# The forward pass of an attention and MLP block: moved loads, reordered copies and filler products at chunk boundaries

## The chip, the cores and the metric

The kernel runs on one core of a Trainium2 chip. The metric is the device time of one execution in microseconds; the time of a kernel is the median of its runs. The engines named below are TensorE (PE: matrix products into PSUM; PEld is its weight load), VectorE (DVE), ScalarE (ACT), GpSimd (POOL) and SyncE (SP). Each engine works through its own instruction stream in order and waits on semaphores. DMAs are issued from the streams of SP and POOL (and ACT in the backward pass).

## The reference

The reference is a transformer block with adaptive layer norm and its gradient: the kernel must return the block's output and the gradients of nine inputs.

```python
mod = (silu(c) @ w_mod).reshape(1, 6, 1, 512)              # sa, ca, ga, sb, cb, gb
h = layernorm(x) * (1 + ca) + sa
x = x + ga * attention(h, wqkv, wo)                        # 32 heads of 16, 2048 tokens, softmax
h = layernorm(x) * (1 + cb) + sb
x = x + gb * (relu(h @ w1 + b1)**2 @ w2 + b2)              # 512 -> 1792 -> 512
out, grads = vjp(block)(grad_out)                          # dx, dwqkv, dwo, dw1, db1, dw2, db2, dc, dw_mod
```

## The kernel before

The program has a short preparation, a forward stage, a stretch that finishes the last chunk, and a backward stage over attention. The change lies in the forward stage alone.

**Units.** Attention scores are computed for 32 heads in 8 groups of 4 (`hg`), the 2048 queries in 4 chunks of 512 (`qc`), the keys in 16 tiles of 128 (`kt`). One unit is one (`qc`, `hg`, `kt`), so there are NF = 512 units, and group boundaries are at the multiples of 16 and chunk boundaries at the multiples of 128. In unit u, `fscore(u)` (line 557) issues four score products on PE into two PSUM pairs `psST` and two exponentials `ET` of 128x1024 on ACT. `fpv(u - 2)` (line 572) issues the four products with the values into the one PSUM bank `oacc`; when a group ends (`kt` = 15, seen in unit `kt` = 1 of the next group) DVE copies `oacc` to `ostage`, POOL casts that to `obf`, and SP later moves rows to `rrows` and a turned copy to `O_un`.

**What is woven in.** `step(u)` (line 1114) adds at most one further product per unit, all through one PSUM bank (`mm()`, tile `pm`): the next piece of `dense_chunk` (line 317), a generator that runs output projection, layer norm, MLP and their backward products for the chunk whose attention has just ended, or one "chain" of weight gradients from the queue `dwq` (`add_chain`, line 226). A number that the generator yields is a count of units to wait. Where a unit has no product, `steady` (line 603) adds two products with zeros, except in the last tile of a group.

**Due times.** `later(lag, f, ...)` puts an issue off by a number of units; `run_due` issues it at the start of its unit. This sets the place of an instruction in its engine's stream, and nothing more: an engine runs on ahead of the units when nothing in its stream makes it wait. DMAs of one queue that use the same one of eight semaphores wait for each other, so each DMA on POOL waits for the landing of the eighth before it.

**Row loads.** `fload` (line 549) loads the keys (`kt_sb`, four DMAs), the queries (`qt_sb`, four) and a bound per query (`m_st`, one) for the next group on the POOL queue, one DMA per unit in chunks 1 to 3, beginning at `kt` = 4 (line 1154). The first score product of the group waits for the last of them.

**A chunk's start.** `ffinish` (line 661), called at the end of unit 8 of the next chunk, turns the softmax sums on PE, and DVE takes their reciprocal and scales four tiles `O_c`. `chunk_loads` (line 282) issues the loads of the chunk's weights and gradients and plans `scaled` (line 305), which multiplies four tiles on POOL into `gf`, whose turned copy `gfT` SP makes.

**Output projection** (lines 345 to 352): four products into `pm`, one per token tile, each followed on DVE by a copy into `a_c`, by `with_input` (two operations) and by `stats` (two). In chunks 0 and 1 a unit without a product lies between them; in chunk 2 they follow unit by unit.

**The chunk's middle** (lines 470 to 502): after the last `pdh` product the four chains of `dwo` are put at the head of `dwq`; SP stores `dx1_c`, turns `da_c` into `daT` and loads `w2_nat` (seven DMAs of 256 KB, tile `wB`); the products with `w2_nat` (line 488) begin after a wait of 5 units. `attn_grad` (line 516) reads `daT` about ten units after that.

**Early units.** `plan_tasks` (line 970) gives the projections of keys and queries to fixed units; `key_norm` of block 1 in units 14, 16, 18 and 20, the bound of the queries from unit 21, and `b1_turn` in unit 22.

Of the kernel before, what the change touches and what calls it, by code (L numbers as in the profile page):

```python
# [20 lines left out]
P = 128  # L21
# [13 lines left out]
def kernel(  # L35
# [110 lines left out]
    with ExitStack() as ph:  # L146
# [142 lines left out]
        def chunk_loads(c):  # L289
# [26 lines left out]
            for ti in range(4):  # L316
                later(5 + ti, scaled, ti)
                later(27 + 2 * ti, sums, ti)
            return L

        def dense_chunk(c, O_c, L):
# [23 lines left out]
            for ti in range(4):  # L345
                pa = mm()
                for oc in range(DC):
                    PE.matmul(pa[:], OT[:, ti, oc, :], L["wo"][:, oc, :], start=(oc == 0), stop=(oc == DC - 1))
                DVE.tensor_copy(a_c[:, ti, :], pa[:])
                with_input(ti)  # L350
                stats(ti)
                yield int(c < QC - 2 and ti < 3)
# [125 lines left out]
            later(5, sp, out1_v[:, ts, :], dx1_c)  # L478
            daT = cb.tile([P, 4, DC, P], BF, name="daT", tag="T4")
            later(5, sp, daT.rearrange("p t o q -> p (t o) q"), flat(da_c), True)  # L480

            w2_nat = load_wB(w2_src, 1, 0.5)
            yield 5
# [119 lines left out]
        def steady(u):  # L603
            if 0 <= u < NF and funits[u][2] < TT - 1:
                for _ in range(2):
                    PE.matmul(fcur["o"][0:DH, :], zeros[:], identb.unsqueeze(1).to_broadcast([P, 4, P]), start=False, stop=False,
                              tile_position=(0, 0), skip_group_check=True)
# [373 lines left out]
        def plan_tasks():  # L981
# [97 lines left out]
            for b, units in ((0, (43, 45, 47, 49)), (1, (14, 16, 18, 20)), (2, (25, 27, 29, 31)), (3, (34, 36, 38, 40))):  # L1079
                for g, u in enumerate(units):  # L1080
                    if b == 0:
                        at(u - 1, lambda g=g: square(T["k"][:, g, :], KTs[0][:, chunk_cols(g)]))
                    at(u, key_norm, b, g)
# [12 lines left out]
            query_bound(21, 0, (1,), (1, 1, 1, 2, 2, 3))  # L1096
            at(22, b1_turn)
# [46 lines left out]
        with ExitStack() as ph2:  # L1144
# [3 lines left out]
            with tc.manual_schedule(engines={PE.engine, ACT.engine, DVE.engine, SP.engine, POOL.engine}):  # L1148
                fh[0, 0] = (qts[0], kts[0])
                for u in range(NF + 2):  # L1150
                    unit[0] = u
                    run_due()
                    if u < NF:
                        if funits[u][2] == (10 if u < 7 * TT else 4) and u + TT < NF:
# [12 lines left out]
                    if u < NF - 4:  # L1167
# [12 lines left out]
                    if not dense and fqueue and fdone and u - 2 >= fdone[0][0]:  # L1180
                        fqueue.pop(0)
                        qc, rr, ou = fdone.pop(0)[1:]
                        ffinish(qc, rr, ou, chunk_loads(qc))
# [979 lines left out]
```

## Time and profile before

| quantity | us |
|---|---|
| median of 3 runs | 2473.05 |
| lowest and highest run | 2471.41 and 2480.04 |
| the profiled execution | 2464.95 |
| its span, first to last instruction | 2463.2 |
| forward stage in it, first to last exponential's start | 37.3 to 995.6 |
| busy in the span: PE, ACT, DVE, POOL | 2295.0, 2299.5, 1813.9, 510.7 |

Times in the rows are microseconds from the first instruction unless ns is written. A row of groups of instructions has: line, engine, operation, output from inputs with shapes and count, then busy time and mean duration in ns of one, then the idle time of the engine just before these instructions and the work whose end released it. A row of the timeline has: start, duration, engine, line, operation, count of merged instructions and, in brackets, the idle time before and its releaser. A row of waits has: the waiting engine, tile and line, what it waited for, then the total, the count and the longest. A row of DMA issues ends with the count, the size of one and the median time from issue to landing. A row of windows has the stretch, its length, busy time (and count) of PE, PEld, DVE, ACT and POOL, the granted PE clock as a share of full speed, the busy share of the DMA engines and GB/s.

### The profile page before, as it was taken

How to read it: one execution, taken by the hardware profiler on the slowest of the kernel's cores; microseconds unless marked ns; L12 is line 12 of the kernel's file. 1: busy time of each engine (PE TensorE's matmuls, PEld its weight loads, DVE VectorE, ACT ScalarE, POOL GpSimd, SP SyncE). 2: the span in 40 equal slices, each digit the busy share in tenths (PEclk: the TensorE clock that was granted, in tenths of full speed). 3: DMA queues.
4: the chain of work that ended last, by engine and by line, in shares of the span. 5: the costliest groups of instructions: out<-in, count | busy, mean ns of one | idle time of the engine just before them, and what ended most of it. 6: DMA issues, size and time to landing. Idle time of an engine off the chain costs nothing. (4 is left out here: it accounts for less than half of the span.)

```text
span 2463.2 us, 49633 instructions
## 1 busy us (share of the span) xinstructions
PE 2295.0 (93%) x18783; PEld 766.5 (31%) x18864; DVE 1813.9 (74%) x2361; ACT 2299.5 (93%) x3581; POOL 510.7 (21%) x692
## 2 busy tenths in 40 slices
PE   8898889988988998899999999999999999999999
PEld 3232223222322332442333333333233333332244
DVE  6655153455435544578999999999999999999985
ACT  8999999999989999638999999999999999999965
POOL 2111222422544353201110101101011010110112
PEclk9999999999999999999999999999999999999999
DMA  4578564366658775979999999999999999999997
GB/s 153 135 161 179 153 134 123 90 175 143 98 87 176 145 118 114 249 235 181 202 202 200 210 202 209 206 209 198 204 207 208 208 213 207 209 205 200 206 226 177
DMA packets 1217027, 440.81 MB, mean 179 GB/s; under 512 B 1093750, under 2 KB 1189620, under 8 KB 1216532
## 3 DMA queue, kind: packets, MB, share of 16 engines
q1 hardware_dynamic: 1171604, 381.60, 82.0%
q0 software_dynamic: 23472, 33.77, 8.0%
q10 hardware_dynamic: 21712, 22.27, 3.7%
q8 instruction: 148, 2.42, 0.4%
q14 instruction: 91, 0.75, 0.1%
HBM read 94.63 MB, written 70.78 MB: 67 GB/s over the span
## 5 line engine op out<-in xcount | busy, mean ns | idle before, releaser
L1641 DVE TENSOR_TENSOR dS_u<-psD_u,E_u 128x1024 bf16<-128x1024 f32 x1024 | 1186.0, 1218 | 59.4 <-PE psD_u L1639 20.3
L569 ACT ACTIVATE ET<-psST 128x1024 bf16<-128x1024 f32 x1024 | 942.1, 1286 | 17.2 <-PE psST L567 16.9
L1625 ACT ACTIVATE E_u<-psS_A 128x512 bf16<-128x512 f32 x768 | 512.9, 668 | 10.4 <-DMA d_st<-dltT 7.5
L1625 ACT ACTIVATE E_u<-psS_B 128x512 bf16<-128x512 f32 x768 | 505.7, 658 | 7.3 <-PE psD_u L1639 2.9
L1639 PE MATMUL psD_u<-iv,ido 32*128 32x512 bf16 x2048 | 408.5, 386 | 0.5 <-DVE dS_u L1641 0.4
L567 PE MATMUL psST<-qt_sb,kt_sb 32*128 32x512 bf16 x2048 | 315.6, 385 | 60.7 <-ACT ET L569 45.5
L1625 ACT ACTIVATE E_u<-psS_C 128x512 bf16<-128x512 f32 x512 | 335.3, 655 | 1.7 <-PE psS_B L1619 0.8
L1619 PE MATMUL psS_A<-ik,iq 32*128 32x512 bf16 x768 | 291.6, 380 | 11.2 <-DVE dwlast L236 1.0
L1619 PE MATMUL psS_B<-ik,iq 32*128 32x512 bf16 x768 | 293.3, 382 | 7.7 <-ACT E_u L1625 0.2
L1726 POOL TENSOR_TENSOR dQacc<-dQacc,dqtmp 128x512 f32<-128x512 f32 x64 | 81.2, 1269 | 840.4 <-ACT dqtmp L1721 779.5
L1619 PEld LDWEIGHTS <-iq 32*128 32x128 bf16 x2048 | 130.3, 91 | 314.8 <-issue 298.7
L1681 PE MATMUL accVK<-dS_u,qz 128*32 128x512 bf16 x2048 | 213.0, 388 | 0.7 <-PE psD_u L1639 0.3
L583 PE MATMUL oacc<-ET,vaug 128*32 128x512 bf16 x2048 | 207.4, 393 | 0.0
L1690 PE MATMUL accVK<-E_u,dOs_tok 128*16 128x512 bf16 x2048 | 201.8, 383 | 0.0
L1619 PE MATMUL psS_C<-ik,iq 32*128 32x512 bf16 x512 | 193.8, 378 | 4.3 <-ACT dqtmp L1721 0.2
L567 PEld LDWEIGHTS <-kt_sb 32*128 32x128 bf16 x2048 | 84.6, 91 | 343.9 <-issue 324.9
L1708 PE MATMUL dqacc<-dsT,KS_tok 128*32 128x512 bf16 x2048 | 146.5, 384 | 15.1 <-DMA dsT<-dS_u 1.3
L250 DVE COPY part<-pm 128x512 f32<-128x512 f32 (+2 forms) x103 | 63.5, 616 | 117.1 <-PE pm L232 104.8
L1785 ACT ACTIVATE dsT<-ptT 128x1024 bf16<-128x1024 bf16 x126 | 144.8, 1149 | 1.9 <-PE ptT L1671 1.7
L1639 PEld LDWEIGHTS <-ido 32*128 32x128 bf16 x2048 | 105.7, 91 | 99.9 <-issue 93.9
L1681 PEld LDWEIGHTS <-qz 128*32 128x32 bf16 x2048 | 58.5, 94 | 177.3 <-issue 162.4
L587 DVE COPY ostage<-oacc 128x512 f32<-128x512 f32 x32 | 22.0, 689 | 101.6 <-PE oacc L583 88.2
(431 smaller groups left out, 2674.1 us busy)
## 6 DMA issues: line engine op xcount, KB each, us to landing
p_st<-part POOLq DMA_DIRECT2D x36, 256.0 KB, 5.1
kt_sb<-qkT_st POOLq DMA_DIRECT2D x124, 64.0 KB, 3.2
wA<-in_B_w_dram SPq DMA_DIRECT2D x28, 256.0 KB, 5.7
wB<-w1T_st SPq DMA_DIRECT2D x21, 256.0 KB, 4.7
wA<-w2T_st SPq DMA_DIRECT2D x21, 256.0 KB, 5.3
wB<-in_B_w_dram SPq DMA_DIRECT2D x21, 256.0 KB, 5.4
p_st<-part POOLq DMA_DIRECT2D x25, 192.0 KB, 4.4
p_st<-part SPq DMA_DIRECT2D x18, 256.0 KB, 2.2
```

The costliest lines, as they stand in the source:

```text
L567: PE.matmul(ps[:, hi, :], kt_sb[r:r + 32, kt * P:(kt + 1) * P], qt_sb[r:r + 32, :], start=True, stop=True, tile_position=(r, 0))
L569: ACT.activation(ET[:, 2 * pair:2 * pair + 2, :], ps[:], AF.Exp, scale=SCALE)
L583: PE.matmul(oacc[32 * hq:32 * hq + 32, :], lhsT, ET[:, hq, :], start=(kt == 0), stop=(kt == TT - 1), tile_position=(0, 32 * hq), skip_grou ...
L1619: PE.matmul(psS[:], st["q"][r:r + 32, qt * P:(qt + 1) * P], st["k"][r:r + 32, kc * 512:kc * 512 + 512], start=True, stop=True, tile_positi ...
L1625: ACT.activation(bst[u][0][:, hq, :], sst.pop((u, hq))[:], AF.Exp, scale=SCALE)
L1639: PE.matmul(psD[:, hi, :], st["do"][r:r + 32, qt * P:(qt + 1) * P], st["v"][r:r + 32, kc * 512:kc * 512 + 512], start=True, stop=True, til ...
L1641: DVE.tensor_tensor(dS_u[:, 2 * pair:2 * pair + 2, :], psD[:], E_u[:, 2 * pair:2 * pair + 2, :], ALU.mult)
L1681: PE.matmul(cur["vk"][32 * hq:32 * hq + 32, :], hst[hg]["qz"][:, qt, hq, :], bst[u][1][:, hq, :], start=(qt == 0), stop=False, tile_positi ...
L1690: PE.matmul(acc[32 * hq:32 * hq + DH, :], dOs_tok[:, qt, (hg * 4 + hq) * DH:(hg * 4 + hq + 1) * DH], E_u[:, hq, :], start=False, stop=(qt ...
L1708: PE.matmul(acc[32 * hq:32 * hq + 32, :], KS_tok[:, kc * 4 + kt, h * DH:h * DH + 32], tT[:, :, hq * 4 + kt, :], start=(kt == 0), stop=(kt ...
L1726: POOL.tensor_tensor(dst2, dst, tmp[:], ALU.add)
L1785: ACT.activation(dst, pt[:], AF.Identity)
```

## The change

Eight places are edited, all in the forward stage. `scaled` is put off from 5 to 14 units after the chunk's start. In the output projection each product is followed on DVE first by its copy, then by `with_input` of the tile before and `stats` of the tile before that; the units between the products of chunks 0 and 1 are gone. The store of `dx1_c` moves from 5 to 9 and the turn to `daT` from 5 to 13 units after the last `pdh` product, the seven `w2` loads are planned one per unit (before: two per unit), and the products with them begin after 6 units. `steady` adds two products of ones into a fresh `pm` where a unit without a product falls on the last tile of a group. `key_norm` of block 1 moves to units 16, 18, 20 and 21, the bound of the queries to 22, `b1_turn` to 21. Row loads from the last group of chunk 0 on begin at `kt` = 2. `ffinish` takes the place of `step` in its unit, so that no chain's product is issued there.

```diff
@@ -314,7 +314,7 @@
             for ti in range(4):
-                later(5 + ti, scaled, ti)
+                later(14 + ti, scaled, ti)
                 later(27 + 2 * ti, sums, ti)
@@ -347,9 +347,14 @@
                 DVE.tensor_copy(a_c[:, ti, :], pa[:])
-                with_input(ti)
-                stats(ti)
-                yield int(c < QC - 2 and ti < 3)
+                if ti > 0:
+                    with_input(ti - 1)
+                if ti > 1:
+                    stats(ti - 2)
+                yield 0
+            with_input(3)
+            stats(2)
+            stats(3)
@@ -475,12 +480,12 @@
             dwq[0:0] = chains
-            later(5, sp, out1_v[:, ts, :], dx1_c)
+            later(9, sp, out1_v[:, ts, :], dx1_c)
             daT = cb.tile([P, 4, DC, P], BF, name="daT", tag="T4")
-            later(5, sp, daT.rearrange("p t o q -> p (t o) q"), flat(da_c), True)
-
-            w2_nat = load_wB(w2_src, 1, 0.5)
-            yield 5
+            later(13, sp, daT.rearrange("p t o q -> p (t o) q"), flat(da_c), True)
+
+            w2_nat = load_wB(w2_src, 1)
+            yield 6
@@ -601,7 +606,11 @@
         def steady(u):
-            if 0 <= u < NF and funits[u][2] < TT - 1:
+            if 0 <= u < NF and funits[u][2] == TT - 1:
+                pz = mm()
+                for _ in range(2):
+                    PE.matmul(pz[:], ones_bf[:], identb.unsqueeze(1).to_broadcast([P, 4, P]), start=True, stop=True)
+            elif 0 <= u < NF:
@@ -1076,7 +1085,7 @@
-            for b, units in ((0, (43, 45, 47, 49)), (1, (14, 16, 18, 20)), (2, (25, 27, 29, 31)), (3, (34, 36, 38, 40))):
+            for b, units in ((0, (43, 45, 47, 49)), (1, (16, 18, 20, 21)), (2, (25, 27, 29, 31)), (3, (34, 36, 38, 40))):
@@ -1093,8 +1102,8 @@
-            query_bound(21, 0, (1,), (1, 1, 1, 2, 2, 3))
-            at(22, b1_turn)
+            query_bound(22, 0, (1,), (1, 1, 1, 2, 2, 3))
+            at(21, b1_turn)
@@ -1151,7 +1160,7 @@
-                        if funits[u][2] == (10 if u < 7 * TT else 4) and u + TT < NF:
+                        if funits[u][2] == (10 if u < 7 * TT else 2) and u + TT < NF:
@@ -1164,7 +1173,11 @@
-                    if u < NF - 4:
+                    if not dense and fqueue and fdone and u - 2 >= fdone[0][0]:
+                        fqueue.pop(0)
+                        qc, rr, ou = fdone.pop(0)[1:]
+                        ffinish(qc, rr, ou, chunk_loads(qc))
+                    elif u < NF - 4:
                         step(u)
@@ -1177,10 +1190,6 @@
-                    if not dense and fqueue and fdone and u - 2 >= fdone[0][0]:
-                        fqueue.pop(0)
-                        qc, rr, ou = fdone.pop(0)[1:]
-                        ffinish(qc, rr, ou, chunk_loads(qc))
```

## The prediction

> **What bounds the kernel now.** I read the page first, then the timeline of ACT over the forward stage, then PE's waits there, then the streams around each hole.
>
> ```profile
> span 2463.2 us, 49633 instructions
> ...
> L569 ACT ACTIVATE ET<-psST 128x1024 bf16<-128x1024 f32 x1024 | 942.1, 1286 | 17.2 <-PE psST L567 16.9
> ...
> p_st<-part POOLq DMA_DIRECT2D x36, 256.0 KB, 5.1
> kt_sb<-qkT_st POOLq DMA_DIRECT2D x124, 64.0 KB, 3.2
> ...
> wB<-in_B_w_dram SPq DMA_DIRECT2D x21, 256.0 KB, 5.4
> ```
>
> The exponentials of the forward stage are busy for 942.1 us out of some 959, and ACT is idle before them for 16.9 us in all, always waiting for a score product. ACT bounds the stage, and 16.9 us is the most that any order of the other work can win there. The timeline says where they lie.
>
> ```profile
> 65.51 234.93 ACT L569 ACTIVATE ET<-psST 128x1024 bf16<-128x1024 f32 x256 [0.60 <-PE psST L567]
> ...
> 531.76 29.44 ACT L569 ACTIVATE ET<-psST 128x1024 bf16<-128x1024 f32 x32 [1.05 <-PE psST L567]
> ...
> 721.27 1.94 ACT L569 ACTIVATE ET<-psST 128x1024 bf16<-128x1024 f32 x2 [5.77 <-PE psST L567]
> 724.12 3.77 ACT L569 ACTIVATE ET<-psST 128x1024 bf16<-128x1024 f32 x4 [0.92 <-PE psST L567]
> 728.36 40.81 ACT L569 ACTIVATE ET<-psST 128x1024 bf16<-128x1024 f32 x44 [0.47 <-PE psST L567]
> ...
> 789.09 1.94 ACT L569 ACTIVATE ET<-psST 128x1024 bf16<-128x1024 f32 x2 [1.22 <-PE psST L567]
> 792.24 140.00 ACT L569 ACTIVATE ET<-psST 128x1024 bf16<-128x1024 f32 x152 [1.21 <-PE psST L567]
> 934.67 1.94 ACT L569 ACTIVATE ET<-psST 128x1024 bf16<-128x1024 f32 x2 [2.43 <-PE psST L567]
> 936.94 1.94 ACT L569 ACTIVATE ET<-psST 128x1024 bf16<-128x1024 f32 x2 [0.33 <-PE psST L567]
> 939.53 1.94 ACT L569 ACTIVATE ET<-psST 128x1024 bf16<-128x1024 f32 x2 [0.65 <-PE psST L567]
> ...
> 989.27 7.44 ACT L569 ACTIVATE ET<-psST 128x1024 bf16<-128x1024 f32 x8 [0.94 <-PE psST L567]
> ```
>
> 234.93 / 256 is 0.918 us an exponential, 1.836 us a unit; from that and the holes before it each hole has its unit: 15, 268, 368 (a group's first), 404, 481 (a group's second), 508. PE's waits over the stage name the causes:
>
> ```profile
> PE psST L567 <- DMA qt_sb<-m_st: 8.7, 2, 5.8
> ...
> PE pm L232 <- DVE part L250: 3.6, 7, 2.0
> ...
> PE pm L808 <- DVE vP L824: 0.8, 1, 0.8
> ```
>
> The two longest are late row loads at group boundaries. Written out unit by unit, the two programs differ in units 14 to 25 and from unit 112 to about 490, and end the forward stage with the same 14 chains left over. So the stretch after it and the backward stage are the same, and the sum is over these holes.
>
> **Row loads two units sooner, and what SP issues beside them (units 356 to 368).** Streams of POOL, of SP, and DMA landings between 690 and 725:
>
> ```profile
> 699.02 0.89 POOL L254 DMA_DIRECT2D p_st<-part  x1 [2.24 <-DVE part L250]
> ...
> 714.89 0.49 POOL L546 DMA_DIRECT2D qt_sb<-qkT_st  x1 [8.99 <-DMA p_st<-part]
> 715.37 0.57 POOL L546 DMA_DIRECT2D qt_sb<-m_st  x1
> ```
>
> ```profile
> 693.23 3.73 SPq L177 DMA_DIRECT2D wB<-in_B_w_dram  x7
> ...
> 697.85 12.98 SPq L177 DMA_TRANSPOSE daT<-a_c  x1
> ```
>
> ```profile
> p_st<-part POOLq DMA_DIRECT2D x4, 256.0 KB, 15.8
> ...
> qt_sb<-qkT_st POOLq DMA_DIRECT2D x4, 16.0 KB, 15.2
> ...
> qt_sb<-m_st POOLq DMA_DIRECT2D x1, 4.0 KB, 5.1
> ```
>
> Four accumulating stores `p_st` share the engines with the `w2` loads, the 512 KB store and the turn to `daT`; they land after 15.8 us (the page's median is 5.1). The fourth `qt_sb` load waits 8.99 us for the first of them (eighth DMA before it on its queue), and `m_st` lands at 715.4 + 5.1 = 720.5. PE was ready 5.8 us earlier, at about 714.7. In the changed order the chunk runs two units ahead at this place, so stores and row loads both come 2 x 1.836 = 3.7 us sooner. SP's part hardly moves: the `w2` loads still stand behind the group's `rrows` and `O_un`, which wait for `ostage`, and nothing that waits stands between them, the store and `daT` on SP, so "later" by units spreads nothing here. If landings stay as long as now, `m_st` lands at 716.8 and 2.1 of the 5.77 us remain; if the earlier stores get out ahead of `daT`, nothing remains. The 0.92 and 0.47 behind it are the catching up and shrink with it. The hole is worth 7.2 us in all; bounds 0 (the engines are drained no sooner) and 7.2; I take 6.0, between 5.0 (3.7 of 5.77 and all of the rest) and 7.2, since the stores move against SP's burst.
>
> **The same at the end of chunk 2 (units 470 to 481).**
>
> ```profile
> 922.57 1.65 POOL L169 TENSOR_TENSOR racc<-racc,dxn 128x512 f32<-128x512 f32 x1
> ...
> 928.41 0.59 POOL L546 DMA_DIRECT2D qt_sb<-m_st  x1
> ```
>
> Here `m_st` stands on POOL behind three row sums (the first is shown), some of which wait for DVE, is issued at 928.4 and holds PE 8.7 - 5.8 = 2.9 us. In the changed order it stands ahead of these sums, so it issues at about 922.6, 5.8 us sooner, and the store and `daT` stand behind the `rrows` of unit 483, after the boundary. All of 2.43 + 0.33 + 0.65 = 3.4 us goes; below that, 0 if the loads still land late; I take 3.4.
>
> **Copies first (units 144 to 148, 272 to 276, 400 to 404).** The streams of PE and DVE at unit 402 and 403:
>
> ```profile
> 787.23 1.02 PE L348 MATMUL pm<-wo_nat,OT 128*128 128x512 bf16 x4 [1.66 <-DVE a_c L349]
> ...
> 789.74 1.86 PE L348 MATMUL pm<-wo_nat,OT 128*128 128x512 bf16 x4 [0.18 <-DVE a_c L349]
> ```
>
> ```profile
> 784.95 0.69 DVE L335 BATCH_NORM_STATS2 st<-x_c 128x6 f32<-128x512 bf16 x1
> 785.68 0.18 DVE L336 BATCH_NORM_AGGREGATE mv<-st 128x2 f32<-128x6 f32 x1
> 785.88 0.69 DVE L587 COPY ostage<-oacc 128x512 f32<-128x512 f32 x1
> 786.49 0.68 DVE L349 CAST a_c<-pm 128x512 bf16<-128x512 f32 x1
> ```
>
> In chunk 2 the copy that frees `pm` stood behind the statistics of the tile before. With the copy first, only `ostage` can stand ahead of it, and that ends before the product does. 1.22 + 1.21 = 2.4 us go. In chunks 0 and 1 the products now follow unit by unit as well: at nothing, because the same order covers them; if it does not, each pays the 2.4 us. Bounds -4.9 and +2.4, I take 2.4. What is late next is the layer norm: two `stats` and one `with_input` lie behind the last copy; the wait of 6 units before the next product covers them.
>
> **Chunk start without a chain (units 136, 264, 392).**
>
> ```profile
> 525.82 4.41 DVE L610 TENSOR_TENSOR O_c<-O_un,r_inv 128x512 bf16<-128x512 bf16 x4
> 530.15 0.55 DVE L250 COPY part<-pm 128x384 f32<-128x384 f32 x1
> ```
>
> DVE scales for 4.41 us, the chain of unit 266 waits behind it for its copy, and the next chain waits 2.0 us (the 2.0 in PE's waits). Without the chain of unit 264 the turn of the sums no longer waits for its copy (0.55 us) nor for its four products (about 1 us, as at 787.23), so the wait falls to some 0.5 us, which the exponentials in hand cover. Worth 1.05; bounds 0 and 1.1; I take 1.0.
>
> **Early units.** `key_norm` no longer follows `value_tile` in unit 14: 0.6 us, bounds 0 and 0.6; in unit 21 `b1_turn` now follows `key_norm` instead, but with a product of 14 columns. I take 0.6.
>
> **At nothing.** The later `gf` products on POOL now stand among the row loads of the next group, nine loads over nine units, 16.5 us, against four products; before, POOL stood waiting for their input. The seven `w2` loads: the last is issued some 3 units, 5.5 us, before its product reads it, against 5.4 us to landing; a landing as slow as the stores' would cost PE what it exceeds. Fourteen new products in `steady`, eight zeros fewer: in units in which PE waits for ACT.
>
> **The clock.** The windows that hold the wait of 2.0 us and the one of 1.66:
>
> ```profile
> 525.00:550.00 25.00, 20.47 (x148) 6.78 (x149) 15.20 (x26) 23.84 (x27) 10.40 (x14) 1.00 0.94 231
> ```
>
> ```profile
> 788.00:792.00 4.00, 3.82 (x22) 0.93 (x20) 3.70 (x9) 1.94 (x2) 3.39 (x8) 0.59 1.07 184
> ```
>
> After the second the granted clock was 0.59 and the product took 1.86 in place of 1.02 us, which makes the second 1.21 us hole; after the first it stayed at 1.00. The Trainium skill's page "TensorE: Matmul & The Clock Gate", section "What's actually happening", says that the clock is halved by default once a window of about 3.4 us lacks activity, and comes back after a busy one. By that rule the chunk starts, which lose their chain and, as `ffinish` has products, their zeros too, could halve the clock; the trace bears it out for the second window and not for the first.
>
> **The sum.** 6.0 + 3.4 + 2.4 + 1.0 + 0.6 = 13.4 us of 16.9; the hole at 508 and small ones stay. The profiled execution took 2464.95 us (its span and 1.75 around it), which would become 2451.5. The median of the runs is 8.1 us above that execution; the same gain taken off it gives 2459.6, or 0.54% less.
>
> **The rivals.**
> Row loads still late: the landings of 15.2 and 15.8 us say that the engines, not the issue, are short, and SP's burst is not spread at unit 356. Against it: at the end of chunk 2 POOL's own stream was the cause. The largest term then falls to 0 and the sum to 7.4: 2465.6. The Trainium skill's page "DMA: Bandwidth & Descriptors", section "Issuing engines are not separate DMA queues", says that queues of several engines run on the same DMA engines; the landings above agree, and it speaks for this rival.
> Copies first does not free PE, as DVE's work for a tile stays the same and longer than a unit (0.68, 0.69, 0.18 and the two of `with_input`): -4.9 in place of +2.4, sum 6.1: 2467.
> The clock halves at the three chunk starts, each with about the hole of 1.21 us, and so at a few boundaries more, some 4 us: sum 9.4: 2463.7. For it the row of 0.59, against it that of 1.00.
> Slower: the `w2` loads. Their slack falls to 5.5 us, and stores in the same burst took 15.8 us. Landing like that, each of three chunks waits 15.8 - 5.5 = 10.3 us on PE: 31 - 13.4 = 17.5 us more, 2490. It decides from 4.5 us of lateness in each chunk. Against it: the loads themselves landed in 5.4 us, and are first on SP's queue.
>
> **How the numbers follow.** Forecast 0.58, row loads late 0.18, copies 0.09, clock 0.08, `w2` late 0.07. A difference of 0.5%, 12.4 us, is about what a measurement of this kernel can tell from no change. The forecast lies just past it; three rivals lie within it, the last beyond on the other side: faster 0.58, same 0.35, slower 0.07. The range takes in the first three rivals (2467 and 2 us) above; below, the whole 16.9 us (2456) and the runs' own distance, 2471.4 to 2480 around 2473, some 5 us: 2451 to 2469. The forecast's own range is 2453 to 2463.
>
> **What would show it.** Right: ACT idle before `ET` at 3 to 5 us, no wait of PE for `m_st` over 2 us, none of L348's successor for `a_c`, the exponentials over by about 983 in place of 996. Wrong: a wait of the `w2` products for `wB`; `m_st` late at a boundary again; a granted clock of 0.5 behind a chunk start; or a backward stage that differs by several us, which nothing here explains.

## The result, and the profile after

The changed kernel took 2465.68 us in the median of 19 runs (2460.05 to 2471.14); the kernel before took 2475.5 us in 19 runs beside them (2467.75 to 2491.84). The ratio is 0.9956, with a 95% interval of 0.9944 to 0.9969: 0.44% faster, clear of the noise. The forecast was 2459.6 us, 0.54% less. The time lies within the range of 2451 to 2469, but 2.7 us past the forecast's own range and on the other side of the mark of 0.5%, in the case to which the prediction gave 0.35.

The profiled execution of the changed kernel took 2467.89 us. Because the kernel before varies by 24 us from run to run, each kernel was profiled once more (below): 2471.05 us for the one before, 2460.22 us for the changed one. First the changed kernel's page and, in its trace, the exponentials by form:

```profile
span 2466.1 us, 49726 instructions
...
L574 ACT ACTIVATE ET<-psST 128x1024 bf16<-128x1024 f32 x1024 | 942.5, 1275 | 12.1 <-PE psST L572 11.6
```

The second profiles, before and changed, in the same view:

```profile
L569 ACT ACTIVATE ET<-psST 128x1024 bf16<-128x1024 f32 x1024 | 942.1, 1314 | 20.1 <-PE psST L567 19.5
```

```profile
L574 ACT ACTIVATE ET<-psST 128x1024 bf16<-128x1024 f32 x1024 | 942.0, 1280 | 4.9 <-PE psST L572 4.4
```

So ACT's idle time before `ET` was 16.9 and 19.5 us before, and 11.6 and 4.4 us after. The timeline of ACT in the changed kernel's first profile shows what is left (the last number is the idle time before the row):

```profile
82.07 5.60 ACT L574 ACTIVATE ET<-psST 128x1024 bf16<-128x1024 f32 x6 [0.91 <-PE psST L572]
88.58 71.60 ACT L574 ACTIVATE ET<-psST 128x1024 bf16<-128x1024 f32 x78 [0.91 <-PE psST L572]
...
721.86 1.94 ACT L574 ACTIVATE ET<-psST 128x1024 bf16<-128x1024 f32 x2 [4.24 <-PE psST L572]
724.78 1.94 ACT L574 ACTIVATE ET<-psST 128x1024 bf16<-128x1024 f32 x2 [0.98 <-PE psST L572]
727.48 92.28 ACT L574 ACTIVATE ET<-psST 128x1024 bf16<-128x1024 f32 x100 [0.76 <-PE psST L572]
...
984.29 7.44 ACT L574 ACTIVATE ET<-psST 128x1024 bf16<-128x1024 f32 x8 [0.94 <-PE psST L572]
```

In the second profile of the changed kernel there is no row at unit 368; in the second of the kernel before that hole, and the two at 400 to 404, are longer than in the first:

```profile
582.04 229.98 ACT L574 ACTIVATE ET<-psST 128x1024 bf16<-128x1024 f32 x250 [0.18 <-PE psST L572]
...
976.54 7.44 ACT L574 ACTIVATE ET<-psST 128x1024 bf16<-128x1024 f32 x8 [0.94 <-PE psST L572]
```

```profile
721.36 1.94 ACT L569 ACTIVATE ET<-psST 128x1024 bf16<-128x1024 f32 x2 [6.81 <-PE psST L567]
724.27 3.77 ACT L569 ACTIVATE ET<-psST 128x1024 bf16<-128x1024 f32 x4 [0.98 <-PE psST L567]
728.87 40.80 ACT L569 ACTIVATE ET<-psST 128x1024 bf16<-128x1024 f32 x44 [0.83 <-PE psST L567]
...
786.42 3.77 ACT L569 ACTIVATE ET<-psST 128x1024 bf16<-128x1024 f32 x4 [1.26 <-PE psST L567]
792.86 141.87 ACT L569 ACTIVATE ET<-psST 128x1024 bf16<-128x1024 f32 x154 [2.66 <-PE psST L567]
...
991.65 7.44 ACT L569 ACTIVATE ET<-psST 128x1024 bf16<-128x1024 f32 x8 [0.94 <-PE psST L567]
```

Sorted by place, idle time of ACT in us (the hole of 0.9 at unit 508, which all four have, and single ones below 0.6 are left out):

| units | before, two profiles | changed, two profiles |
|---|---|---|
| 15 | 0.6, 0.6 | 0, 0 |
| 24 and 27 | 0, 0 | 1.8, 0.6 |
| 66, 82, 98 | 0, 0 | 0.8, 0.8 |
| 268 | 1.1, 0 | 0, 0 |
| 292 to 295, 420 to 423 | 0, 0 | 1.5, 1.4 |
| 368 to 371 | 7.2, 8.6 | 6.0, 0 |
| 400 to 404 | 2.4, 3.9 | 0, 0 |
| 480 to 482 | 3.4, 3.6 | 0, 0 |

The last eight exponentials begin at 989.27 and 991.65 us before, at 984.29 and 976.54 after: a gain of 5.0 us in the first pair and 15.1 in the second (7.4 and 12.7 if the pairs are crossed). The medians' 9.8 us lie between. Behind the exponentials the changed profiles are longer: from those rows to the end of the span the two profiles before took 1473.9 and 1477.7 us, the changed ones 1481.8 and 1481.9. That stretch has the same work in both. The ten other kernels below, also with the same work there, took anything from 1477.2 to 1485.5 us, three of them 1477.2 to 1478.8, so it is not shown that the change lengthens it.

### The profile page after: what moved, and what is told of

It reads as the page before. It is cut to its first block, busy times and chain, and to the rows that moved or that the text cites. A ratio compares the mean times of both kernels' runs of the same rounds, so it can differ in the third digit from the quotient of the medians.

```text
span 2466.1 us, 49726 instructions
## 1 busy us (share of the span) xinstructions
PE 2303.2 (93%) x18870; PEld 766.2 (31%) x18870; DVE 1826.6 (74%) x2361; ACT 2300.5 (93%) x3581; POOL 511.5 (21%) x692
## 5 line engine op out<-in xcount | busy, mean ns | idle before, releaser
L574 ACT ACTIVATE ET<-psST 128x1024 bf16<-128x1024 f32 x1024 | 942.5, 1275 | 12.1 <-PE psST L572 11.6
L1628 PE MATMUL psS_A<-ik,iq 32*128 32x512 bf16 x768 | 292.1, 380 | 11.4 <-ACT E_u L1634 1.0
L1735 POOL TENSOR_TENSOR dQst<-dQacc,dqtmp 128x512 bf16<-128x512 f32 x32 | 40.6, 1270 | 265.7 <-ACT dqtmp L1730 265.7
```

The source lines that it names most:

```text
L574: ACT.activation(ET[:, 2 * pair:2 * pair + 2, :], ps[:], AF.Exp, scale=SCALE)
L1628: PE.matmul(psS[:], st["q"][r:r + 32, qt * P:(qt + 1) * P], st["k"][r:r + 32, kc * 512:kc * 512 + 512], start=True, stop=True, tile_positi ...
L1735: POOL.tensor_tensor(dst2, dst, tmp[:], ALU.add)
```

## The experiments

All ratios are to the kernel before, run on the same chip beside the kernel in question.

**Both kernels again.** No edit; one execution each.

> The kernel before once more, unchanged, to see what of its holes repeats. In the two profiled executions compared so far the exponentials end only 5.0 us sooner after the change (989.3 against 984.3 at the start of the last row of exponentials), while the medians differ by 9.8 us. Theory 1 (the gain is made of holes in the forward stage, and the first look at the kernel before was one with short holes): the idle time of ACT before ET is above 16.9 us here, 20 us or more, with the excess at the group boundaries 368 and 481 whose loads land late. Theory 2 (the rest of the gain does not lie in the forward stage, and the backward stage drifts by several us from one execution to the next): ACT is idle before ET for 16 to 18 us again, and the distance from the last exponential to the end differs from the first look (1466 us) by several us.

> The changed kernel once more, unchanged. Theory 1: idle time of ACT before ET again near 11.6 us, or lower, with the hole at unit 368 (4.2 us in the first look) varying by a microsecond or more, as it is a matter of landings, and the two holes of 0.91 us at units 24 and 27 the same, as they are a matter of PE and DVE. Theory 2: the forward stage within 0.5 us of the first look, and the distance from the last exponential to the end other than 1474 us by several us.

These are the second profiles shown above: 2471.05 and 2460.22 us. The hole at unit 368 was closed or not without any edit. What differed is the landing. DMA issues between 690 and 725 us, first the changed kernel's first profile, then its second (number issued, KB each, median us from issue to landing):

```profile
p_st<-part POOLq DMA_DIRECT2D x4, 256.0 KB, 13.9
...
qt_sb<-m_st POOLq DMA_DIRECT2D x1, 4.0 KB, 15.4
```

```profile
p_st<-part POOLq DMA_DIRECT2D x4, 256.0 KB, 7.2
...
qt_sb<-m_st POOLq DMA_DIRECT2D x1, 4.0 KB, 5.6
```

POOL issued `m_st` early both times, in the first profile here:

```profile
705.57 0.54 POOL L551 DMA_DIRECT2D qt_sb<-m_st  x1
```

That is 9.8 us sooner than the 715.37 of the kernel before. With 5.6 us to landing it was in time; with 15.4 it came at 721, where it had come before.

**Without the accumulating stores of chunk 1.** The stores of `p_st` of the four `dwo` chains are left out, and so is that part of the output.

```diff
-                else:
+                elif not (c == 1 and idx >= FC + 4 * NS):
```

> The changed kernel without the four accumulating stores of the gradient of wo in chunk 1 (that part of the gradient of wo is left out of its output). Theory A (the accumulating stores and the turn to daT slow each other in the DMA engines, and the row loads behind the stores on POOL's queue land with them): the load of m_st lands within 6 us in place of 15.4, the hole at unit 368 goes from 4.2 us to under 0.5, and the turn occupies SP's queue for about 5 us in place of 12.6. Theory B (the bytes of SP's burst, w2, store and turn, are what drains late): the hole stays at 3 us or more, since these are all still there.

2464.17 us, one execution, and no hole at 368; `m_st` landed after 5.4 us, and the turn held SP for 6.42 us in place of 12.60 and 10.77. The changed kernel's second profile had no hole either, with the stores, and in the run with the whole chunk start undone (below) the turn took 6.42 us with the stores. So this one execution is no evidence for or against them.

**The turn of `da` ahead of the `w2` loads.**

```diff
-            later(9, sp, out1_v[:, ts, :], dx1_c)
             daT = cb.tile([P, 4, DC, P], BF, name="daT", tag="T4")
-            later(13, sp, daT.rearrange("p t o q -> p (t o) q"), flat(da_c), True)
+            later(1, sp, daT.rearrange("p t o q -> p (t o) q"), flat(da_c), True)
+            later(9, sp, out1_v[:, ts, :], dx1_c)
```

> The changed kernel with the turn to daT issued 1 unit after the last product of that part in place of 13, ahead of the w2 loads on SP: the turn is through before the accumulating stores begin. Theory A (stores and turn slow each other): the hole at unit 368 goes to under 1 us, the turn takes SP about 5 us; the w2 loads come some 5 us later and may cost PE up to 2 us before their first product. Net 3 to 4 us sooner than the changed kernel, ratio to the kernel before about 0.994. Theory B (only the sum of bytes matters): the hole at 368 stays at 3 us or more and the w2 loads are later on top, ratio about 0.997.

2479.36 us (2475.03 to 2494.26, 10 runs), ratio 1.0015 (0.9994 to 1.0036): the whole gain is gone. PE's waits over the forward stage of this kernel (us in total, times, longest):

```profile
PE pm L493 <- DMA wB<-in_B_w_dram: 11.1, 9, 2.9
```

This wait is absent in both profiles of the changed kernel. PE waits for the `w2` loads in the middle of all three chunks (ACT's holes are at units 235 to 237, 361 to 365 and 485 to 487), and the last eight exponentials come 18.8 us later than in the changed kernel's second profile. It is the mechanism of the rival on the slower side: it exists, and the changed order, in which the `w2` loads go ahead of the turn on SP, stays clear of it.

**Row loads two units later again.**

```diff
-                        if funits[u][2] == (10 if u < 7 * TT else 2) and u + TT < NF:
+                        if funits[u][2] == (10 if u < 7 * TT else 4) and u + TT < NF:
```

> The changed kernel with one edit undone: the row loads of a group begin at key tile 4 again, two units later. Theory A (the step of the prediction: the sooner issue of m_st is what shortens the hole at unit 368): the hole returns to 5.8 to 7 us as in both profiles of the kernel before, with PE waiting 4 to 7 us for m_st, and the median lies 4 to 6 us above the changed kernel's 2465.7. Theory B (the moved chunk start, which spreads the w2 loads, the turn of da and the store of da_c, decides when the DMA engines are drained; the issue does nothing): the hole stays between 0 and 4.4 us, as in the two profiles of the changed kernel, and the median stays within 2 us of 2465.7. Theory C (the landing varies from execution to execution, and the sooner issue buys slack against it): no hole in a good execution, a longer one in a bad, median 1 to 4 us up and the spread of the times wider.

2476.64 us (2469.48 to 2484.21, 12 runs), ratio 1.0001 (0.9985 to 1.0018): more than any theory allowed. At 368 ACT was idle for only 1.6 us in the profile. New holes stood at units 148, 276 and 404, one in each chunk, each of 2.2 to 2.9 us of idle time. The streams of PE, DVE and POOL at the third of them:

```profile
791.40 1.02 PE L348 MATMUL pm<-wo_nat,OT 128*128 128x512 bf16 x4 [2.64 <-DVE a_c L349]
```

```profile
786.61 0.41 DVE L330 TENSOR_TENSOR atmp<-a_c,modbc 128x512 bf16<-128x512 bf16 x1
787.06 3.69 DVE L331 TENSOR_TENSOR x_c<-atmp,x_c 128x512 bf16<-128x512 bf16 x1
790.67 0.68 DVE L349 CAST a_c<-pm 128x512 bf16<-128x512 f32 x1
```

```profile
787.39 1.16 POOL L306 TENSOR_TENSOR gf_c<-g_c,modbc 128x512 bf16<-128x512 bf16 x1
788.49 0.53 POOL L551 DMA_DIRECT2D kt_sb<-qkT_st  x1
789.04 1.16 POOL L306 TENSOR_TENSOR gf_c<-g_c,modbc 128x512 bf16<-128x512 bf16 x1
```

An addition that took 0.42 us in the kernel before took 3.69 here. It ends half a microsecond after the second `gf` product on POOL does (789.04 + 1.16), as if it had run only then. It stands between two copies of `a_c`, so PE waits. The moved `gf` products are one of the parts of the change that the prediction set "at nothing".

**`gf` alone back at lag 5, and the whole chunk start undone.** The first edit is the first pair of lines, the second all of them.

```diff
-                later(14 + ti, scaled, ti)
+                later(5 + ti, scaled, ti)
...
-            later(9, sp, out1_v[:, ts, :], dx1_c)
-            later(13, sp, daT.rearrange("p t o q -> p (t o) q"), flat(da_c), True)
-            w2_nat = load_wB(w2_src, 1)
-            yield 6
+            later(5, sp, out1_v[:, ts, :], dx1_c)
+            later(5, sp, daT.rearrange("p t o q -> p (t o) q"), flat(da_c), True)
+            w2_nat = load_wB(w2_src, 1, 0.5)
+            yield 5
```

> The changed kernel with one number undone: the gf products on POOL at lag 5 again instead of 14; the later store and turn, the w2 loads and the six units stay. Theory A (gf among the row loads holds DVE: an add of a_c and ga took 3.26 us beside them in the changed kernel and 3.7 with the row loads at key tile 4, against 0.42 in the kernel before): these adds fall back to 0.4 to 0.9 us at all three chunk starts and the time is 0.5 to 3 us below the changed kernel's 2465.7, as with the whole chunk start undone (2462.5). Theory B (the whole start had to be undone for its 3 us, gf is beside the point): the adds fall back, the time stays within 1 us of 2465.7. The squares of the hidden layer stay at about 720 ns in either, since what lies beside them are the sums, not gf.

> The changed kernel with the chunk start undone: gf on POOL, the store of da_c and the turn of da at lag 5 again, the w2 loads at half pace, one unit less ahead of the first product. Theory A (the sooner row loads alone were enough): the hole at unit 368 stays between 0 and 4.4 us and the median within 2 us of 2465.7. Theory B (the spreading of the chunk start is what lets the row loads land): the hole is back at 5 to 7 us and the median is 4 to 6 us up. The holes of 0.3 us at units 292 to 295 stay if gf has no part in them.

`gf` alone: 2463.77 us (6 runs), ratio 0.9952 (0.9936 to 0.9967). The whole start: 2462.49 us (6 runs), 0.9939 (0.9920 to 0.9959). Neither can be told from the changed kernel's 0.9956; the spread of the chunk loads and of the turn has bought nothing that shows. The additions by form, in the changed kernel and with `gf` back (busy us, mean ns):

```profile
L330 DVE TENSOR_TENSOR atmp<-a_c,modbc 128x512 bf16<-128x512 bf16 x12 | 13.8, 1147 | 0.0
```

```profile
L330 DVE TENSOR_TENSOR atmp<-a_c,modbc 128x512 bf16<-128x512 bf16 x12 | 4.9, 410 | 0.0
```

The blocked additions are there in the changed kernel, but with the row loads at key tile 2 they fall behind a copy that PE has already got. In chunk 1 of the changed kernel, for example, an addition of 3.23 us begins at 545.27 us, behind the copy for which PE waits. Their cost is hidden by a matter of two units.

**Row loads later and `gf` back, together.** Both edits above.

> Row loads at key tile 4 again and gf at lag 5 again, the rest as changed. Theory A (of the 11 us that the row loads alone cost when undone, the holes of 2.5 to 3.2 us at units 148, 276 and 404 came from gf, which fell two units out of step with the copies; the row loads' own worth is the hole at 368): the holes at 148, 276 and 404 go, the one at 368 is 1.8 to 7 us, median 2467 to 2472. Theory B (the row loads themselves, by their issues on POOL, hold the copies): holes of over 2 us stay at 148, 276 and 404, median about 2476.

2468.46 us (2461.82 to 2472.39, 8 runs), ratio 0.9961 (0.9944 to 0.9977), apart from the 1.0001 with `gf` among the loads. The holes at 148, 276 and 404 are gone. The one at 368 is back in the profile, on ACT and, as its cause, on POOL:

```profile
722.89 1.94 ACT L574 ACTIVATE ET<-psST 128x1024 bf16<-128x1024 f32 x2 [7.17 <-PE psST L572]
```

```profile
708.88 0.49 POOL L551 DMA_DIRECT2D qt_sb<-qkT_st  x1 [5.20 <-DMA kt_sb<-qkT_st]
715.86 0.48 POOL L551 DMA_DIRECT2D qt_sb<-qkT_st  x1 [6.49 <-DMA p_st<-part]
...
717.46 0.58 POOL L551 DMA_DIRECT2D qt_sb<-m_st  x1
```

POOL stands twice for older transfers, 5.20 and 6.49 us, before it may issue the next load. Against `gf` alone the row loads are worth 4.7 us in the median (2468.46 to 2463.77), but the intervals of the two ratios overlap (0.9944 to 0.9977, 0.9936 to 0.9967), so the size is not shown. The eight times fall into two groups, four from 2461.8 to 2466.9 and four from 2470.0 to 2472.4. The profile with the hole of 7.17 us is of the run of 2465.50 us, one of the lower four: what parts the groups is not known.

**Output projection in the old order, alone and with the chunk end.** The first kernel undoes the order of the copies and the idle units of chunks 0 and 1; the second also moves `ffinish` behind the chain again, and has `gf` at lag 5.

```diff
-                if ti > 0:
-                    with_input(ti - 1)
-                if ti > 1:
-                    stats(ti - 2)
-                yield 0
-            with_input(3)
-            stats(2)
-            stats(3)
+                with_input(ti)
+                stats(ti)
+                yield int(c < QC - 2 and ti < 3)
```

> The changed kernel with the order of the output projection undone (each copy followed by its own add and statistics, and three idle units again in chunks 0 and 1). Theory A (the step of the prediction): the two holes at units 403 and 404 return, 2.4 us in the profile before and up to 4 us in its second profile, and the time is 2 to 4 us up. Theory B (the order does not matter; the holes at 403 and 404 were a late landing before it): the holes stay away and the time is within 1 us. Beside it the squares of the hidden layer on DVE (sT from rT) took 574 ns in the mean before and 721 after, since four sums of g on POOL now lie beside the first hidden products: if the three units by which these products came sooner are the cause, their mean falls back to about 574 ns and the holes of 0.3 us at units 292 to 295 go, worth 1.1 us; if the row loads are, it stays at 721.

> The order of the output projection and the chunk end undone together, gf at lag 5; row loads at key tile 2, the later store and turn and the w2 loads as changed. The two edits act at different places. Theory A (the terms of the prediction): 1.2 to 2.8 us of holes come back at units 403 and 404, and 3.4 to 4.5 us at 480 to 483; median 4 to 7 us above that of the run with gf alone put back. Theory B (the holes at 403 and 404 followed from the late start after the hole at 368, as in the profile in which both are long): nothing comes back at 403 and 404 when 368 is closed, 480 to 483 come back, median 3 to 4 us up. Theory C (the hole at 368 is closed only because the projection ran three units sooner): it is back with 4 to 6 us and the median is 8 to 12 us up.

Alone: 2473.17 us (2469.59 to 2480.20, 12 runs), ratio 0.9986 (0.9973 to 0.9999). With the chunk end: 2476.37 us (2462.81 to 2488.21, 12 runs), 0.9996 (0.9977 to 1.0015). The second kernel's ACT timeline, and its PE waits from 500 to 830 us:

```profile
534.34 46.17 ACT L569 ACTIVATE ET<-psST 128x1024 bf16<-128x1024 f32 x50 [1.69 <-PE psST L567]
...
787.54 1.94 ACT L569 ACTIVATE ET<-psST 128x1024 bf16<-128x1024 f32 x2 [2.02 <-PE psST L567]
789.76 29.44 ACT L569 ACTIVATE ET<-psST 128x1024 bf16<-128x1024 f32 x32 [0.28 <-PE psST L567]
```

```profile
PE pm L348 <- DVE a_c L349: 1.7, 1, 1.7
```

The hole for a copy of `a_c` is back with 2.0 + 0.3 us, though unit 368 is closed in this profile: it comes from the order, not from a late start. In the projection's own run it is back with 1.1 + 0.2 us. The hole at 268 is back with 1.7 us in the second kernel, and not in the first. At 480 to 482 nothing comes back, and nothing did with the row loads undone. In the projection's own run PE waited 5.1 us for `m_st` at 368; it was issued at 706.81 us, about as early as in the changed kernel, and took 14.6 us to land. The second kernel's profile was its fastest run, 13.6 us under its median, so no profile shows what its slow runs wait for.

The squares of the hidden layer did not fall back to 574 ns in either kernel (708 and 710); with the row loads at key tile 4 they did nearly, to 598. By the alternative set down before the run, the row loads are the cause and not the sooner projection.

**Early units in the old order.**

```diff
-            for b, units in ((0, (43, 45, 47, 49)), (1, (16, 18, 20, 21)), (2, (25, 27, 29, 31)), (3, (34, 36, 38, 40))):
+            for b, units in ((0, (43, 45, 47, 49)), (1, (14, 16, 18, 20)), (2, (25, 27, 29, 31)), (3, (34, 36, 38, 40))):
...
-            query_bound(22, 0, (1,), (1, 1, 1, 2, 2, 3))
-            at(21, b1_turn)
+            query_bound(21, 0, (1,), (1, 1, 1, 2, 2, 3))
+            at(22, b1_turn)
```

> The changed kernel with the order of the early units undone (key_norm of head block 1 at units 14, 16, 18, 20, the bound's rows from 21, b1_turn at 22). Theory A (the moved key work crowds DVE beside the bound and leaves PE idle long enough for its clock to halve): the holes at units 24 and 27 (0.9 each beyond a pair in one profile, 1.2 at 27 alone in the other, 2.45 and 1.18 against the common pace) go, the hole of 1.0 at unit 15 returns, so the unit at 82 us starts 0 to 1.5 us sooner and the median is 0 to 1.5 us below the changed kernel's. Theory B (the holes at 24 and 27 come from elsewhere): they stay, the hole at 15 returns, and the time is 0.5 to 1 us up.

2462.81 us (2458.84 to 2470.31, 6 runs), ratio 0.9945 (0.9923 to 0.9967), not to be told from the changed kernel. The hole at 15 came back with 0.6 us, the one at 27 shrank to 0.2, the one at 24 stayed with 0.5. Unit 32 starts 59.1 us after unit 0 in both profiles before, 60.2 here, and 60.6 and 59.3 in the changed kernel's two. What goes with the hole at 24 is the granted clock. From 76 to 84 us it was 1.00 in both profiles before and in the changed kernel's second, which have no such hole; in the changed kernel's first, here and in the nine other kernels of this section it fell in that stretch, to between 0.62 and 0.91 in the first 4 us, and all of them have the hole. In these units only two filling products in unit 17 still differ between this kernel and the one before. Whether they make the clock fall was not tried.

**What the runs speak against, taken out.** `gf` at lag 5 and the early units as before, the sums of `g` on POOL behind the hidden squares, and no filling product beside three token tiles.

```diff
-                later(27 + 2 * ti, sums, ti)
+                later(51 + ti, sums, ti)
...
-            if 0 <= u < NF and funits[u][2] == TT - 1:
+            if 0 <= u < NF and funits[u][2] == TT - 1 and u not in (63, 79, 95):
...
-            elif 0 <= u < NF:
+            elif 0 <= u < NF and funits[u][2] < TT - 1:
...
```

> The changed kernel with what the runs speak against taken out: the early units as before, gf at lag 5, the sums of g moved from lag 27 to 51 (behind the hidden squares, where DVE reads the sums of TensorE and not two bf16 operands from memory), and no filling product in the three last units of a group in which a token tile is copied (units 63, 79, 95) nor in the units of the last key tile but those. Expected beside the changed kernel: the squares at 430 to 450 ns instead of 720 and the holes of 0.3 us at 292 to 295 and 420 to 423 gone (2 us); the holes of 0.35, 0.2 and 0.2 us at 66, 82 and 98 gone (0.5 to 0.8); 24 and 27 gone and 15 back (0.6 to 1.2); the adds at 0.42 us (0 to 3). Sum 3 to 7 us: 2458.5 to 2462.5. If the holes close and the time does not move, other work behind them is late.

2460.44 us (2453.62 to 2467.42, 6 runs), ratio 0.9937 (0.9918 to 0.9956). The median is 5.2 us below the changed kernel's, but the intervals overlap; it is not shown to beat it, nor the kernel with the whole chunk start undone (0.9939). The squares by form, changed and here, and ACT here:

```profile
L407 DVE TENSOR_TENSOR sT<-rT 128x512 bf16<-128x512 bf16 x42 | 30.3, 721 | 1.4
```

```profile
L407 DVE TENSOR_TENSOR sT<-rT 128x512 bf16<-128x512 bf16 x42 | 17.9, 425 | 1.4
```

```profile
82.94 1.94 ACT L574 ACTIVATE ET<-psST 128x1024 bf16<-128x1024 f32 x2 [0.97 <-PE psST L572]
85.07 870.60 ACT L574 ACTIVATE ET<-psST 128x1024 bf16<-128x1024 f32 x948 [0.18 <-PE psST L572]
957.08 13.20 ACT L574 ACTIVATE ET<-psST 128x1024 bf16<-128x1024 f32 x14 [1.41 <-PE psST L572]
```

The middle row holds 948 exponentials without a gap that the view would split: the holes at 66, 82, 98, 292 to 295, 368 and 420 to 423 are gone. A new one of 1.41 us stands near the end, at unit 499; there the granted clock was 0.67 from 953 to 957 us, and four products of line 525 took 1.73 us where the same four took 1.02 in the changed kernel's first profile.

## Why the prediction was right and wrong

**Row loads two units sooner: right in kind, the size not shown.** Predicted 6.0 us (0 to 7.2); measured 4.7 in the median with `gf` out of the way, with overlapping intervals. The step made one time of it, and it is two: 6.0 us of idle time remain in one profile of the changed kernel and none in the other. The rival "row loads still late" is thus true in some executions. That the median of 2465.68 us is that rival's 2465.6 is chance: in the second profile, 2460.22 us, the loads were in time. The step had named the case that came, in which the earlier stores get out ahead of the turn. POOL's order of loads and stores at this place is the same before and after, but the first store now goes out ahead of SP's turn, where it had gone out behind it (699.02 against 697.85 us). In the first profile of the changed kernel the store goes out at 697.48 and the turn at 699.08 us; the second profile on POOL, on SP and on POOL again:

```profile
696.16 0.89 POOL L254 DMA_DIRECT2D p_st<-part  x1 [1.93 <-DVE part L250]
```

```profile
697.59 10.77 SPq L177 DMA_TRANSPOSE daT<-a_c  x1
```

```profile
703.45 0.49 POOL L551 DMA_DIRECT2D qt_sb<-qkT_st  x1 [0.42 <-DMA p_st<-part]
703.93 0.54 POOL L551 DMA_DIRECT2D qt_sb<-m_st  x1
```

POOL's wait for that store fell from 8.99 to 0.75 and 0.42 us, and `m_st` went out 9.8 and 11.4 us sooner, not the 3.7 of the step's first case. What the step's sum did not hold is that a load issued that early can still take 15.4 us to land. Why it does so in one execution and not in another stays open.

**End of chunk 2: right, 3.4 us predicted and 3.4 and 3.6 gone.** (The hole is at unit 480, a group's first, not 481.) The step gives two reasons, the sooner `m_st` and the store and the turn behind the boundary, and the runs show that each is enough beside the rest of the change. With the row loads at key tile 4 again `m_st` stands behind the row sums again and goes out at 929.02 us, no sooner than the 928.41 before, and yet no hole is there, as it lands sooner. DMA issues from 920 to 932 us, in the kernel before and in that run:

```profile
qt_sb<-m_st POOLq DMA_DIRECT2D x1, 4.0 KB, 5.7
```

```profile
qt_sb<-m_st POOLq DMA_DIRECT2D x1, 4.0 KB, 2.0
```

The turn was issued at 927.47 us in the kernel before, ahead of that load, and at 941.01 in that run. With the whole chunk start undone the turn is ahead of the boundary again, at 920.24 us, but `m_st` goes out before it, at 914.84, and no hole is there either.

**Copies first: right, 2.4 us predicted.** Undone, 1.4 and 2.3 us of holes come back at 403 and 404 in the two profiles, with the wait for `a_c`. Undone alone, the edit costs 7.5 us in the median. Its profile shows a hole of 7.3 us at 368 beside the 1.4, with the late `m_st`; whether the later chunk makes that landing late, or it was one of the late executions, is not shown.

**Chunk start without a chain: right that the hole goes, wrong about DVE.** 1.0 predicted; the hole was 1.1 us in one profile before and absent in the other, and 1.7 come back at unit 268 with the chain. The step took the 4.41 us of scaling for DVE's own work. At this chunk start they are 2.50 us in every profile without the chain and 3.46 in the second profile before. In the kernel before, the four `gf` products on POOL begin 1.1 us after the scaling has begun:

```profile
526.93 5.41 POOL L306 TENSOR_TENSOR gf_c<-g_c,modbc 128x512 bf16<-128x512 bf16 x4 [16.09 <-DMA g_c<-in_grad_out_dram]
```

With `gf` at lag 5 again and no chain, the scaling on DVE is over before POOL begins:

```profile
527.90 2.50 DVE L619 TENSOR_TENSOR O_c<-O_un,r_inv 128x512 bf16<-128x512 bf16 x4
```

```profile
531.21 4.49 POOL L306 TENSOR_TENSOR gf_c<-g_c,modbc 128x512 bf16<-128x512 bf16 x4 [15.50 <-DMA g_c<-in_grad_out_dram]
```

So the chain's place let `gf` on POOL run into the scaling. Whether the later `gf` alone would have closed the hole, with the chain kept, was not tried.

**Early units: the hole at 15 went, and 0.6 to 1.8 us came at 24 and 27.** Net that is 0 to 1.2 us lost where 0.6 was to be won. The old order put back shrank the hole at 27 to 0.2 us and left the one at 24, which goes with the granted clock. The term looked at the unit that lost work and not at those that got it.

**"At nothing": wrong twice, and one effect left out.** The step set the `gf` products against POOL's own queue only. They hold DVE, and that costs 8.2 us, most of the gain, when they fall between two copies (2476.64 against 2468.46 with the row loads later, intervals apart); in the changed kernel they fall elsewhere. The filling products cost 0.8 us where a token tile's copy holds `pm`: there PE did not wait for ACT alone. The effect left out is on the squares of the hidden layer: they went from 574 to 721 ns, with 1.5 us of holes at 292 to 295 and 420 to 423. The sooner row loads on POOL do it, since these alone, put back, bring 598 ns and no such holes. With the sums of `g` on POOL moved away the squares take 425, so these sums are what DVE meets, a little in the kernel before and more in the changed one.

**The clock.** The clock's rival came with its sign and without its price. In each profile of the changed kernel the granted clock fell behind one of the chunk starts, to 0.66 from 772 to 776 us in the first and to 0.73 from 288 to 292 us in the second, and ACT shows no hole there.

**The sum.** Of 13.4 us the forward stage gave 5.0 and 15.1 in the two pairs of profiles. The first is short by the late landing (6.0 us) and by the new holes, the second exceeds it because the kernel before also varies: 16.9 and 19.5 us of holes. Reading the gain off one profile of a kernel whose holes depend on landings was the weak point: that profile, 2464.95 us, lies below all 19 runs of the kernel before. That a sum of terms, some too high and some left out, ends within 4 us of the medians' 9.8 is in part luck. The prediction had named a backward stage that differs by several us as a sign that something is not explained; 4 to 8 us more stand there in these profiles, and other kernels show as much spread. Its other signs: ACT idle for 3 to 5 us and the exponentials over by about 983 held in the second profile (4.4; 976.54 + 7.44 = 984.0) and not in the first (11.6; 991.7), where PE waited 4.7 us for `m_st`. No product waited for `wB`.

**The rival on the slower side** did not occur, but the turn put first showed its price: 11.1 us of waits for `wB`.

## What to carry to other kernels

When work is moved to another engine's idle time, look at what other engines do in those units, not only at its own queue: here products on POOL stretched an addition on DVE to nearly nine times its length, and the loss showed only when another edit shifted the copies by two units. A busy time in a profile can hold such a wait: DVE's 4.41 us of scaling were 2.50 without it. A late load that lands in 5.6 us in one execution and in 15.4 in the next is a distribution and not a number: profile such a kernel more than once before a gain is taken off it. And undoing edits one at a time can lose the whole gain for several of them at once (11.0 us, 7.5 us), so single worths aren't to be added.

## What the runs showed of the hardware

DVE operations with two bf16 operands took 0.42 us alone, 1.4 beside one POOL operation of 1.17, and 3.2 to 3.7 beside a train of POOL products with DMA issues between them. The middle case, on DVE and POOL in the changed kernel's second profile:

```profile
574.22 1.43 DVE L407 TENSOR_TENSOR sT<-rT 128x512 bf16<-128x512 bf16 x1
```

```profile
574.18 1.17 POOL L169 TENSOR_TENSOR racc<-racc,g_c 128x512 f32<-128x512 f32 x1
```

The Trainium skill's page "SBUF — State Buffer", section "Who interferes with whom", says that a DVE instruction with two SBUF inputs contends with a GpSimd one that reads SBUF, and that the later one is held until the other ends. The 1.4 us agree with it. The 3.69 us of the run with the row loads later do not follow from it alone: by the record the addition begins 0.33 us ahead of the first product, and it was not let in during the 0.53 us in which POOL issued a DMA between two products, but only after the second. POOL's DMA issues without products did not hold it: 0.42 us beside nine of them in the run with `gf` at lag 5.

The granted clock fell at 76 to 84 us in the changed kernel's first profile though PE was busy for about three quarters of the window and more:

```profile
76.00:80.00 4.00, 2.98 (x20) 0.85 (x20) 1.41 (x4) 4.00 (x6) 0.47 (x1) 0.80 0.58 163
80.00:84.00 4.00, 3.92 (x24) 0.98 (x23) 2.42 (x5) 3.10 (x5) 1.45 (x4) 0.77 0.48 121
```

The columns are the window, its length, busy us (and instructions) of PE, of its weight load, DVE, ACT and POOL, the granted clock, the DMA share and GB/s. In its second profile the clock stayed at 1.00 there with 3.01 us of PE in the first of these windows: nearly the same load falls on either side from one execution to the next.

One DMA of 4 KB took 5.6 or 15.4 us to land in the same program, behind the same stores of 256 KB.
